# Six tiles of scores in one run, the fourth in the banks of attn @ v

## The chip, the cores and the metric

The kernel runs on one core of a Trainium2 chip. Time is the device time of one execution in microseconds (us); lower is better. The engines are called by their names in the profile: PE (TensorE, the matmuls), PEld (its weight loads), DVE (VectorE), ACT (ScalarE), POOL (GpSimd) and SP (SyncE, which issues the DMAs). SBUF is the working memory, PSUM the memory of eight banks into which matmuls write.

## The reference

All inputs are f32. For each of 8 batches and 12 heads, with 448 rows of 64:

```python
scores = scale * np.matmul(q, k.transpose(0, 1, 3, 2)) - np.log(S)
attn = 1.0 / (1.0 + np.exp(-scores))
out = np.matmul(attn, v)
x = out.transpose(0, 2, 1, 3).reshape(B * S, H * D)     # 3584 x 768
h = np.maximum(x @ moe_w_in, 0.0)                       # 768 x 2048, given as f64
result = (h * h) @ moe_w_out                            # 2048 x 768, given as f64
```

The two weight matrices come as 8-byte numbers and are turned into f32 on the chip.

## The kernel before

The kernel has an attention stage and an MLP stage. The change touches the attention stage and the names of some PSUM banks in the MLP.

**Pairs and blocks.** The 96 heads are 48 *pairs* of two heads, numbered n = 0 to 47; one pair's q and k are one tile x of 128 partitions by 2 x 448 (`load_pair`, 448 KB). `block(ps, d)` works on two pairs, n = 2d and n + 1, for d = 0 to 23. All of the attention stage stands under a manual schedule: on each engine, instructions run in the order in which the program writes them.

**Scores.** To keep f32 accuracy with the faster fp32r matmul, each x is *split* into a high part (a cast, line 254, DVE) and a low part (x minus the high part, line 255, DVE). Scores of a pair (`scores`, line 263) are three tiles of 128 keys by 2 heads by 448 queries. Each tile is two PSUM banks and takes three passes (high x high, low x high, high x low), each pass two matmuls, one for each head, which run side by side (line 272). There are three such tiles in PSUM, tag "sc", six banks. ACT turns every tile into attention weights with a sigmoid (line 260). 448 keys leave a rest of 64 for each pair; `scores_rest` (line 282) computes the rest of the next block's two pairs in one tile, from x that isn't split.

**attn @ v.** `attn_v_rest` (line 293) opens the sums of both pairs in two single banks, tag "single", with the part of the rest; `attn_v` (line 304) adds the three tiles of one pair. `put_x` (line 312) copies a finished sum out of its bank to a tile xo, on DVE for the even pair and on ACT for the odd one (`scalar=True`). For the first two batches xo is kept in SBUF, otherwise it is stored to HBM by a DMA.

**Weights beside it.** Between the scores the f64 weights are converted: `weights_words` (ACT, lines 145 and 146, called words) and `weights_join`, which is either a *join* (three DVE operations at lines 150, 151 and 154, then an add on POOL at line 157) or, each third step, the *sums* of four blocks (DVE, lines 166 to 169) with two stores. The steps are spread over the pairs: step k belongs to pair k * 45 // 43, so nearly each pair has one step. `weights_join` also issues the load of a later chunk. The dictionary `PIECES` adds work at the end of blocks 13, 15, 17, 19, 21, 22 and 23: `make` (pieces 1, 2, 3, 6) splits x operands of the MLP, the high part by ACT (line 327) and the low part by DVE (line 328), in three parts; pieces "t1" to "t3" are three subtractions on DVE (line 353).

**The order of one block before**, d > 0, as each engine sees its part:

```python
put(n - 1, True)                    # ACT copies the odd pair of the block before
score(ps, n, xs[n])                 # PE: three tiles; ACT: three sigmoids
weights_of(weights_join, n - 1)     # DVE, POOL: first slot
split_ahead(n + 2)                  # DVE
rest[d + 1] = scores_rest(...)      # PE, ACT
pav[n], pav[n + 1] = attn_v_rest(...)
score(ps, n + 1, xs[n + 1])         # PE: three tiles more
weights_of(weights_join, n)         # second slot
...                                 # words, stores of xo
attn_v(n, ...); split_ahead(n + 3); attn_v(n + 1, ...)
pieces_of(...); put(n)              # DVE copies the even pair
```

**The MLP.** Two products by Strassen's scheme with seven products each, four groups of tokens. Sums of kind "a" and "b" lie in six banks of a second pool, which takes the room of the score tiles; sums of kind "c" (hc in the first product, oc in the second) lie in the two single banks.

Of the kernel before, what the change touches and what calls it, by code (L numbers as in the profile page):

```python
# [68 lines left out]
def sigmoid_attention_relu2_mlp(  # L69
# [181 lines left out]

    def split_pair(b, p, x):
        hi, lo = op2(f"qh_{b}_{p}", F32R), op2(f"ql_{b}_{p}", F32R)
        nc.vector.tensor_copy(out=hi, in_=x)  # L254
        nc.vector.tensor_sub(out=lo, in0=x, in1=hi.bitcast(F32))  # L255
        return hi, lo

    def sigmoid(name, sc):
# [3 lines left out]

    def scores(ps, b, p, x, passes=((0, 0), (1, 0), (0, 1))):

        out = []
        for t in range(NT):
            sc = ps.tile([P, 2, 512], F32, tag="sc", bufs=3, name=f"sc_{b}_{p}_{t}")[:, :, :S]
            ks = slice(t * P, (t + 1) * P)
            for n, (kp, qp) in enumerate(passes):
                for j in range(2):  # L270
                    rows = slice(j * D, (j + 1) * D)
                    nc.tensor.matmul(  # L272
                        sc[:, j],
                        x[kp][rows, 1, ks],
                        x[qp][rows, 0],
                        start=(n == 0),
                        stop=(n == len(passes) - 1),
                    )
            out.append(sigmoid(f"at_{b}_{p}_{t}", sc))
        return out  # L280

    def scores_rest(ps, d, xs):

        sc = ps.tile([P, 2, 512], F32, tag="sc", bufs=3, name=f"sr_{d}")[:, :, :S]
        for r, x in enumerate(xs):
            for j in range(2):
                rows = slice(j * D, (j + 1) * D)
                nc.tensor.matmul(  # L288
                    sc[r * KR : (r + 1) * KR, j], x[rows, 1, NT * P :], x[rows, 0], start=True, stop=True
                )  # L290
        return sigmoid(f"rest_{d}", sc)

    def attn_v_rest(d, rest, vt):

        pavs = [single(f"pav_{2 * d + r}") for r in range(2)]
        for r in range(2):
            for j in range(2):
                rows, columns = slice(r * KR, (r + 1) * KR), slice(j * D, (j + 1) * D)
                nc.tensor.matmul(  # L299
                    pavs[r][columns], vt[rows, 2 * NT, columns], rest[rows, j], start=True, stop=False  # L300
                )
        return pavs
# [85 lines left out]

    ps1 = ctx.enter_context(tc.tile_pool(name="ps1", bufs=2, space=PSUM))
    warm = op2("warm").rearrange("p a s -> p (a s)").bitcast(BF16)  # L390
# [32 lines left out]

    def block(ps, d):

# [3 lines left out]
        more = n + 2 <= last  # L429
        for m in (n + 4, n + 5):  # L430
            load(m)
# [5 lines left out]
        if d == 0:  # L437
            split_ahead(1)
            score(ps, 0, (x[0],), ((0, 0),))
            rest[0] = scores_rest(ps, 0, (x[0], x[1]))  # L440
            score(ps, 1, xs[1])
        else:
            put(n - 1, True)
            score(ps, n, xs[n])
            weights_of(weights_join, n - 1)
        split_ahead(n + 2)
        if more:
            rest[d + 1] = scores_rest(ps, d + 1, (x[n + 2], x[n + 3]))
        pav[n], pav[n + 1] = attn_v_rest(d, rest.pop(d), vt[d])
        if d > 0:  # L450
            score(ps, n + 1, xs[n + 1])
        weights_of(weights_join, n)
        weights_of(weights_words, n)
        weights_of(weights_words, n + 1)
# [13 lines left out]

    def split_ahead(n):
        if n <= last:  # L470
            xs[n] = split_pair(*pairs[n], x[n])

    def score(ps, n, *args):
        at[n] = scores(ps, *pairs[n], *args)

# [25 lines left out]


    def single(name):
        return ps1.tile([P, 512], F32, tag="single", bufs=2, name=name)[:, :S]

# [11 lines left out]
    def gemm1(g, ops, weights, between):  # L517
# [25 lines left out]
        def run(n, i):  # L543
# [70 lines left out]
    def gemm2(g, blocks, operands1, weights1, ahead):  # L614
# [47 lines left out]
        for at, n in enumerate(order):  # L662
# [5 lines left out]
            for e in range(NE):  # L668
                if n in (1, 7, 2):
                    banks[k, e] = (single if k == "c" and e < 2 else bank)(f"o{k}_{g}_{e}")  # L670
                for i in range(NI):
# [27 lines left out]
    with tc.manual_schedule():  # L699
        with tc.tile_pool(name="ps", bufs=3, space=PSUM) as ps:  # L700
# [8 lines left out]
            for h in range(2):  # L709
                f64[0, h] = load_chunk(*todo[0], h)  # L710
            for d in range(len(pairs) // 2 - 2):
                block(ps, d)
# [4 lines left out]
            block(ps, len(pairs) // 2 - 2)  # L717
# [73 lines left out]
```

## Time and profile before

| | us |
|---|---|
| median of 3 runs | 1080.39 |
| the runs | 1080.41, 1080.39, 1079.15 |
| profiled execution, its own time | 1079.62 |
| its span in the profile | 1077.8 |
| PE busy | 1071.5 |
| DVE busy | 800.7 |
| ACT busy | 610.1 |
| POOL busy | 68.0 |

The profile is one execution; its times count from the first instruction, and what lies between the span and the execution's own time is before and after the program's instructions. A row of the order of time gives the start in us, the length in us, the engine and its line in the kernel, the operation, which tile it writes and which it reads, the size, and how many instructions of the same kind are merged (x2). What stands in brackets at its end is how long the engine had been idle and what released it. A row of a group gives the number of instructions, then the busy time in us, the mean ns of one, and the idle time ahead of them. Lengths of two matmuls overlap, since matmuls are pipelined: the distance from start to start is what a matmul costs. PE busy near 100% therefore doesn't say that PE works at its peak, and a wait of PE shows as a start that comes late.

### The profile page before, as it was taken

To read this page: it belongs to the slowest core of one execution; us is meant where nothing else is said; L and a number is where in the kernel's file an instruction comes from. 1 tells how busy PE (TensorE), PEld (TensorE's weight loads), DVE (VectorE), ACT (ScalarE), POOL (GpSimd) and SP (SyncE) were. 2 spreads that over 40 slices of the span, in tenths; PEclk is the share of its full clock that TensorE was granted. 3 is DMA by queue.
4 is the path that set the end of the run, shared out by engine and by line. 5 is a ranking of instruction groups with operands and counts; after the bars stand their busy time and mean duration, and the time that the engine had idled before them with its cause. 6 is when DMAs were issued, how large, how long until landed. Compare 5 with 4: busy or idle time off the path is not lost.

```text
span 1077.8 us, 14887 instructions
## 1 busy us (share of the span) xinstructions
PE 1071.5 (99%) x5859; PEld 887.3 (82%) x5859; DVE 800.7 (74%) x867; ACT 610.1 (57%) x752; POOL 68.0 (6%) x40
## 2 busy tenths in 40 slices
PE   9999999999999999999999999999999999999998
PEld 4555555546999999999999999999999999999997
DVE  6999899996787996825579975456896935579941
ACT  7888888876555664534454753344565623355721
POOL 1222223220020000000000000000000000000000
PEclk9999999999999999999999999999999999999999
DMA  9989999964654435543343464333345633333441
GB/s 370 387 307 336 347 354 340 352 226 137 228 198 154 143 117 176 194 140 103 103 120 108 127 233 161 110 116 105 90 141 187 209 94 114 123 101 115 143 143 52
DMA packets 82294, 196.80 MB, mean 183 GB/s; under 512 B 6576, under 2 KB 56624, under 8 KB 82224
## 3 DMA queue, kind: packets, MB, share of 16 engines
q1 hardware_dynamic: 82224, 195.85, 52.8%
q8 instruction: 46, 0.75, 0.3%
q14 instruction: 24, 0.20, 0.0%
HBM read 154.53 MB, written 41.29 MB: 182 GB/s over the span
## 4 chain that ended last, share of the span: by engine, by line
PE 91%; DVE 7%; issue 2%; ACT 0%; ACTq 0%; DVEq 0%
PE ha L513 22%; PE oa L513 22%; PE hb L513 11%; PE ob L513 11%; PE pav L308 6%; PE sc L272 6%; PE hc L513 5%; PE oc L513 5%; DVE ql L255 2%; PE sr L288 1%; PE pav L299 1%; DVE qh L254 1%; DVE a L154 1%; DVE a L151 1%; DVE a L150 0%
## 5 line engine op out<-in xcount | busy, mean ns | idle before, releaser
L235 DVE TENSOR_TENSOR w_1l<-w_1l,w_1h 128x1536 fp32r<-128x1536 f32 x60 | 105.3, 1756 | 63.2 <-ACT w_1h L234 62.7
L260 ACT ACTIVATE at<-sc 128x896 f32<-128x896 f32 x144 | 121.8, 920 | 20.8 <-PE sc L272 20.8
L541 ACT COPY s<-ha 128x448 f32<-128x448 f32 x96 | 51.0, 532 | 145.7 <-PE ha L513 131.3
L308 PE MATMUL pav<-at,v 128*64 128x448 f32 x576 | 113.5, 543 | 0.0
L234 ACT CAST w_1h<-w_1l 128x1536 fp32r<-128x1536 f32 x60 | 88.8, 1480 | 19.3 <-DMA w_1l<-w 19.2
L255 DVE TENSOR_TENSOR ql<-x,qh 128x896 fp32r<-128x896 f32 x47 | 94.5, 2011 | 1.7
L308 PEld LDWEIGHTS pav<-at,v 128*64 128x64 f32 x576 | 39.1, 137 | 63.6 <-issue 63.4
L235 DVE TENSOR_TENSOR w_5l<-w_5l,w_5h 128x1152 fp32r<-128x1152 f32 x32 | 43.3, 1355 | 46.5 <-ACT w_5h L234 46.5
L157 POOL TENSOR_TENSOR a<-a,f 128x768 int32<-128x768 int32 x28 | 58.6, 2093 | 177.4 <-ACT xo L315 58.7
L234 ACT CAST w_0h<-w_0l 128x1536 fp32r<-128x1536 f32 x28 | 41.5, 1481 | 47.9 <-DMA w_0l<-w 47.9
L235 DVE TENSOR_TENSOR w_0l<-w_0l,w_0h 128x1536 fp32r<-128x1536 f32 x28 | 49.1, 1754 | 13.5 <-ACT w_0h L234 13.4
L272 PE MATMUL sc<-qh 64*128 64x448 f32 x282 | 56.9, 398 | 0.0
L537 DVE SCALAR_TENSOR_TENSOR g<-g 128x896 f32<-128x896 f32 x48 | 54.1, 1128 | 1.3
L272 PEld LDWEIGHTS sc<-qh 64*128 64x128 f32 x282 | 26.6, 184 | 34.3 <-ACT at L260 15.5
L573 DVE TENSOR_TENSOR g<-hb,s 128x448 f32<-128x448 f32 x32 | 19.9, 622 | 44.7 <-PE hb L513 44.6
L272 PE MATMUL sc<-ql,qh 64*128 64x448 f32 x282 | 51.9, 362 | 0.0
L272 PE MATMUL sc<-qh,ql 64*128 64x448 f32 x282 | 51.7, 361 | 0.0
L234 ACT CAST w_5h<-w_5l 128x1152 fp32r<-128x1152 f32 x32 | 37.1, 1159 | 24.8 <-DMA w_5l<-w 24.8
L659 ACT COPY t<-oa 128x448 f32<-128x448 f32 x36 | 19.1, 530 | 40.1 <-PE oa L513 39.9
L567 ACT ACTIVATE g<-ha 128x448 f32<-128x448 f32 x32 | 17.4, 544 | 33.8 <-PE ha L513 33.8
L513 PE MATMUL oa<-o_2l,w_1h 128*128 128x448 f32 x96 | 35.1, 365 | 0.0
L513 PE MATMUL oa<-o_2h,w_1l 128*128 128x448 f32 x96 | 35.1, 365 | 0.0
(520 smaller groups left out, 3029.8 us busy)
## 6 DMA issues: line engine op xcount, KB each, us to landing
w_1l<-w SPq DMA_DIRECT2D x60, 768.0 KB, 4.4
x<-qk SPq DMA_DIRECT2D x48, 448.0 KB, 6.0
w_0l<-w SPq DMA_DIRECT2D x28, 768.0 KB, 4.5
f<-w_in SPq DMA_DIRECT2D x16, 768.0 KB, 9.2
w_5l<-w SPq DMA_DIRECT2D x32, 384.0 KB, 4.0
v<-v SPq DMA_DIRECT2D x24, 448.0 KB, 6.8
w<-s SPq DMA_DIRECT2D x14, 768.0 KB, 7.8
outT<-o SPq DMA_DIRECT2D x47, 224.0 KB, 2.0
```

The costliest lines, as they stand in the source:

```text
L157: nc.gpsimd.tensor_tensor(out=wb, in0=wb, in1=t.bitcast(I32)[:, :, 0], op=ALU.add)
L234: nc.scalar.copy(out=hi, in_=raw)
L235: nc.vector.tensor_sub(out=lo, in0=raw, in1=hi.bitcast(F32))
L255: nc.vector.tensor_sub(out=lo, in0=x, in1=hi.bitcast(F32))
L260: nc.scalar.activation(at, sc, AF.Sigmoid, bias=NEG_LOG_S, scale=SCALE)
L272: nc.tensor.matmul(sc[:, j], x[kp][rows, 1, ks], x[qp][rows, 0], start=(n == 0), stop=(n == len(passes) - 1),)
L308: nc.tensor.matmul(pav[columns], vt[:, n % 2 * NT + t, columns], at[t][:, j], start=False, stop=(t == NT - 1))
L513: nc.tensor.matmul(out, a[:, c], b, start=first and n == 0, stop=last and n == 2, skip_group_check=True)
L537: nc.vector.scalar_tensor_tensor(out=t, in0=t, scalar=0.0, in1=t, op0=ALU.max, op1=ALU.mult)
L541: nc.scalar.copy(out=s, in_=banks["a", i])
L573: nc.vector.tensor_add(out=tile_of("21", i), in0=out, in1=snaps[2, i])
L659: nc.scalar.copy(out=s, in_=banks["a", e])
```

## The change

It does five things in the attention stage.

- Scores of both pairs of a block come in one run of six tiles, `score(n)` and `score(n + 1)`; the rest of scores, the opening of attn @ v and attn @ v follow.
- The two single banks become one tile of two banks, tag "duo", of which there is one. It holds the sums of attn @ v of both pairs, and, before these are opened, the first tile of the odd pair's scores, the fourth of the run.
- Both copies of x of a block stand in the next block, behind the first slot's join or sums and the first half of a split, and both are on DVE.
- The split is taken apart into `high` and `low`, and goes one pair further ahead: block d splits pairs n + 3 and n + 4 instead of n + 2 and n + 3. In the first slot the two copies stand between high and low. Block 0 splits pairs 1 to 4. Loads of x go one pair further ahead too, with pair 4 loaded ahead of block 0.
- In the MLP, sums of kind "c" take their banks from the same tile of two banks: hc for two products of neighbouring i together, oc for e = 0 and 1.

```diff
-    def split_pair(b, p, x):
-        hi, lo = op2(f"qh_{b}_{p}", F32R), op2(f"ql_{b}_{p}", F32R)
-        nc.vector.tensor_copy(out=hi, in_=x)
-        nc.vector.tensor_sub(out=lo, in0=x, in1=hi.bitcast(F32))
-        return hi, lo
+    def score_tile(name):
+        return ps.tile([P, 2, 512], F32, tag="sc", bufs=3, name=name)[:, :, :S]
 
-    def scores(ps, b, p, x, passes=((0, 0), (1, 0), (0, 1))):
+    def scores(b, p, x, passes=((0, 0), (1, 0), (0, 1))):
...
-            sc = ps.tile([P, 2, 512], F32, tag="sc", bufs=3, name=f"sc_{b}_{p}_{t}")[:, :, :S]
+            sc = (duo if p % 2 and t == 0 else score_tile)(f"sc_{b}_{p}_{t}")
...
     def attn_v_rest(d, rest, vt):
 
-        pavs = [single(f"pav_{2 * d + r}") for r in range(2)]
+        sums = duo(f"pav_{d}")
+        pavs = [sums[:, r] for r in range(2)]
...
-    def block(ps, d):
+    def block(d):
         n = 2 * d
         more = n + 2 <= last
-        for m in (n + 4, n + 5):
+        for m in (n + 5, n + 6):
             load(m)
...
         if d == 0:
-            split_ahead(1)
-            score(ps, 0, (x[0],), ((0, 0),))
-            rest[0] = scores_rest(ps, 0, (x[0], x[1]))
-            score(ps, 1, xs[1])
+            for m in (1, 2, 3):
+                high(m)
+                low(m)
+            score(0, (x[0],), ((0, 0),))
+            rest[0] = scores_rest(0, (x[0], x[1]))
         else:
-            put(n - 1, True)
-            score(ps, n, xs[n])
             weights_of(weights_join, n - 1)
-        split_ahead(n + 2)
+            high(n + 3)
+            put(n - 2)
+            put(n - 1)
+            low(n + 3)
+            score(n, xs[n])
+        score(n + 1, xs[n + 1])
         if more:
-            rest[d + 1] = scores_rest(ps, d + 1, (x[n + 2], x[n + 3]))
+            rest[d + 1] = scores_rest(d + 1, (x[n + 2], x[n + 3]))
         pav[n], pav[n + 1] = attn_v_rest(d, rest.pop(d), vt[d])
-        if d > 0:
-            score(ps, n + 1, xs[n + 1])
         weights_of(weights_join, n)
+        high(n + 4)
+        low(n + 4)
         weights_of(weights_words, n)
         weights_of(weights_words, n + 1)
...
         attn_v(n, pav[n], at[n], vt[d])
-        split_ahead(n + 3)
         attn_v(n + 1, pav[n + 1], at[n + 1], vt[d])
         pieces_of(*PIECES.get(d, ()))
-        put(n)
...
+    def high(n):
+        if n <= last:
+            xs[n] = op2(f"qh_{n}", F32R), op2(f"ql_{n}", F32R)
+            nc.vector.tensor_copy(out=xs[n][0], in_=x[n])
+
+    def low(n):
+        if n <= last:
+            nc.vector.tensor_sub(out=xs[n][1], in0=x[n], in1=xs[n][0].bitcast(F32))
...
-    def single(name):
-        return ps1.tile([P, 512], F32, tag="single", bufs=2, name=name)[:, :S]
+    def duo(name):
+        return ps1.tile([P, 2, 512], F32, tag="duo", bufs=1, name=name)[:, :, :S]
...
-                banks[k, i] = (single if k == "c" else bank)(f"h{k}_{g}_{i}")
+                if k != "c":
+                    banks[k, i] = bank(f"h{k}_{g}_{i}")
+                elif i % 2 == 0:
+                    two = duo(f"hc_{g}_{i}")
+                    banks[k, i], banks[k, i + 1] = two[:, 0], two[:, 1]
...
             for h in range(2):
                 f64[0, h] = load_chunk(*todo[0], h)
+            load(4)
...
-            block(ps, len(pairs) // 2 - 1)
+            block(len(pairs) // 2 - 1)
+            put(last - 1)
             put(last, True)
```

More of the change, by code (lines that the diff above doesn't have):

```diff
@@ L280, in scores, with scores_rest @@
         return out
-    def scores_rest(ps, d, xs):
-        sc = ps.tile([P, 2, 512], F32, tag="sc", bufs=3, name=f"sr_{d}")[:, :, :S]
+    def scores_rest(d, xs):
+        sc = score_tile(f"sr_{d}")
         for r, x in enumerate(xs):
@@ L387, in x_operands @@
         }
-    ps1 = ctx.enter_context(tc.tile_pool(name="ps1", bufs=2, space=PSUM))
+    ps1 = ctx.enter_context(tc.tile_pool(name="ps1", bufs=1, space=PSUM))
     warm = op2("warm").rearrange("p a s -> p (a s)").bitcast(BF16)
@@ L467, in load, with score @@
             x[n] = load_pair(*pairs[n])
-    def split_ahead(n):
+    def high(n):
         if n <= last:
-            xs[n] = split_pair(*pairs[n], x[n])
-    def score(ps, n, *args):
-        at[n] = scores(ps, *pairs[n], *args)
+            xs[n] = op2(f"qh_{n}", F32R), op2(f"ql_{n}", F32R)
[3 more added lines that the diff above has]
+            nc.vector.tensor_sub(out=xs[n][1], in0=x[n], in1=xs[n][0].bitcast(F32))
+    def score(n, *args):
+        at[n] = scores(*pairs[n], *args)
     def put(n, scalar=False):
@@ L669, in gemm2 @@
                 if n in (1, 7, 2):
-                    banks[k, e] = (single if k == "c" and e < 2 else bank)(f"o{k}_{g}_{e}")
+                    if k != "c" or e == 2:
+                        banks[k, e] = bank(f"o{k}_{g}_{e}")
+                    elif e == 0:
+                        two = duo(f"oc_{g}")
+                        banks[k, 0], banks[k, 1] = two[:, 0], two[:, 1]
                 for i in range(NI):
@@ L710, in sigmoid_attention_relu2_mlp @@
                 f64[0, h] = load_chunk(*todo[0], h)
+            load(4)
             for d in range(len(pairs) // 2 - 2):
-                block(ps, d)
+                block(d)
                 if d == KEPT * NP // 2:
@@ L716, in sigmoid_attention_relu2_mlp @@
             load_first(0, False)
-            block(ps, len(pairs) // 2 - 2)
+            block(len(pairs) // 2 - 2)
             load_first(0, True)
```

## The prediction

> **What bounds the kernel now.** I read the busy time of the engines over the attention stage first, then the order of time of TensorE (PE), VectorE (DVE), GpSimd (POOL), ScalarE (ACT) and the DMA queue (SP) in one pair of pairs, a block. In the order of time the columns are start, length in us, engine, line. Only this stage changes its pace; it runs from 16.75 us, the start of block 1, to 256.87 us, the first matmul of the MLP.
>
> ```profile
> 16.75:256.87 240.12, 238.45 (x1742) 123.57 (x1740) 222.57 (x271) 196.31 (x248) 58.61 (x28) 1.00 0.89 329
> ```
>
> The columns after the span are the busy us of PE, its weight loads, DVE, ACT and POOL, then the granted clock, 1.00. PE is full and DVE has 222.57 of 240.12: two engines close to their limit. Block 18 on PE, and the few rows beyond it that I need:
>
> ```profile
> 16.75 0.47 PE L272 MATMUL sc<-qh 64*128 64x448 f32 x2
> ...
> 192.99 0.47 PE L272 MATMUL sc<-qh 64*128 64x448 f32 x2
> 193.29 0.36 PE L272 MATMUL sc<-qh,ql 64*128 64x448 f32 x2
> ...
> 194.70 0.37 PE L272 MATMUL sc<-ql,qh 64*128 64x448 f32 x2
> 195.01 0.98 PE L288 MATMUL sr<-x 64*64 64x448 f32 x8
> 195.81 0.93 PE L299 MATMUL pav<-rest,v 64*64 64x448 f32 x8
> 196.67 0.47 PE L272 MATMUL sc<-qh 64*128 64x448 f32 x2
> ...
> 198.69 4.73 PE L308 MATMUL pav<-at,v 128*64 128x448 f32 x24
> 203.35 0.47 PE L272 MATMUL sc<-qh 64*128 64x448 f32 x2
> ...
> 239.64 0.98 PE L299 MATMUL pav<-rest,v 64*64 64x448 f32 x8 [1.13 <-DVE xo L317]
> ...
> 247.23 0.48 PE L272 MATMUL sc<-qh 64*128 64x448 f32 x2
> ...
> 256.87 0.47 PE L513 MATMUL ha<-x_0h,w_1h 128*128 128x448 f32 x1
> ```
>
> A block takes 203.35 - 192.99 = 10.36 us; the last one, without a rest of scores, 256.87 - 247.23 = 9.64. 22 blocks and the last make 237.6 of 240.1 us, so PE waits some 2.4 us in all now. The row at 239.64 shows what for: a copy of x that DVE made late. That copy may come up to 2.8 us into the next block before PE minds.
>
> DVE beside it, from a join of weight words (line 150 on) to the next group:
>
> ```profile
> 195.26 0.55 DVE L150 TENSOR_SCALAR a<-a 128x768 f32<-128x768 f32 x1
> ...
> 197.31 0.62 DVE L254 CAST qh<-x 128x896 fp32r<-128x896 f32 x1
> 197.97 2.64 DVE L255 TENSOR_TENSOR ql<-x,qh 128x896 fp32r<-128x896 f32 x1
> 200.53 0.55 DVE L150 TENSOR_SCALAR a<-a 128x768 f32<-128x768 f32 x1
> ...
> 205.80 0.61 DVE L317 COPY xo<-pav 128x448 f32<-128x448 f32 x1
> 206.34 0.54 DVE L166 TENSOR_TENSOR s<-a 128x384 f32<-128x384 f32 x1
> ...
> 208.32 0.62 DVE L254 CAST qh<-x 128x896 fp32r<-128x896 f32 x1
> 208.98 1.09 DVE L255 TENSOR_TENSOR ql<-x,qh 128x896 fp32r<-128x896 f32 x1
> 209.99 0.55 DVE L150 TENSOR_SCALAR a<-a 128x768 f32<-128x768 f32 x1
> ```
> ```profile
> 197.63 2.03 POOL L157 TENSOR_TENSOR a<-a,f 128x768 int32<-128x768 int32 x1 [9.04 <-DMA w<-s]
> ```
>
> The subtraction of a split (line 255) takes 1.09 us alone and 2.64 behind a join, where POOL's add is under way until 199.66. So a join with its split costs 200.53 - 195.26 = 5.27 us of DVE, a group of sums with its split 209.99 - 206.34 = 3.65, a copy of x 0.54.
>
> **The gain on PE.** T is the start of a block's scores. Pairs of score matmuls follow each other by (194.70 - 193.29) / 7 = 0.201; the first takes 0.30 (192.99 to 193.29) and the last hands over after 0.31. Two runs of nine pairs cost 2 x 2.02 = 4.04 us, one run of eighteen 0.30 + 16 x 0.201 + 0.31 = 3.83. The rest of scores (0.80), the rest of attn @ v (0.86) and attn @ v (4.66) keep their prices, as a seam is only moved. A block comes to 10.15, 0.21 less: 22 blocks give 4.6 us. Work on weights, x operands and the whole MLP keep their amount; the hc and oc pairs of banks are asked for again only several products (1.8 us each) after their adds, so I cost them at nothing. load(4) ahead of block 0 stays behind the same transfers, and v and the next words go one x-load later (448 KB, 1.4 us at the 329 GB/s of the first row), and are first read in block 1, more than that after they land.
>
> **What the fourth tile waits for.** It lies in the banks of attn @ v, so PE may write it only once both copies of x of the block before are done. It starts at T + 0.30 + 8 x 0.201 = T + 1.91. A copy lasts 0.61, so with a hand-over of under 0.1 the second copy must start by T + 1.23; it can't start before T + 0.1, when attn @ v has ended. Thus the window on DVE shrinks from some 4.5 us (2.3 before T to 2.1 after) to 1.1, and both copies are now DVE's, where ACT took one. Everything after the copy on DVE, and PE's tiles five and six, the rest and attn @ v, queue behind it.
>
> From the start of a join to the second copy it is 2.05 (195.26 to 197.31) + 0.66 + 0.54 = 3.25 us; from the sums 1.98 + 0.66 + 0.54 = 3.18. Behind a join the two copies fill time in which the subtraction stood still for POOL anyway (197.97 to 199.66), so join and split with two copies remain 5.27. This asks that a copy from PSUM runs beside POOL's add. Below is the nearest row: a DVE operation reading PSUM, begun 0.25 us after POOL and not stretched. I take that, at no cost; the other bound, a copy held until POOL ends, moves the second copy by 199.66 + 0.54 - 195.26 - 3.25 = 1.7 us.
>
> ```profile
> 328.06 1.03 POOL L157 TENSOR_TENSOR b<-b,fd 128x384 int32<-128x384 int32 x1 [5.28 <-issue]
> ```
> ```profile
> 328.31 0.62 DVE L573 TENSOR_TENSOR g<-hb,s 128x448 f32<-128x448 f32 x1 [0.38 <-PE hb L513]
> ```
>
> Now from second copy to second copy. After a join in the block's first slot, 5.27 - 3.25 = 2.02 us of that slot remain, after sums 0.54 + 1.01 = 1.55. Steps run sums, join, join, and a block takes two: first slot join, then join, then sums: 2.02 + 5.27 + 3.18 = 10.47; first slot sums, then join, join: 1.55 + 5.27 + 3.25 = 10.07; first slot join, then sums, join: 2.02 + 3.65 + 3.25 = 8.92. Together 29.46 against 3 x 10.15 = 30.45: it fits on the mean. But a join can't start before ACT has read its words, and ACT does these after seven sigmoids:
>
> ```profile
> 193.89 2.54 ACT L260 ACTIVATE at<-sc 128x896 f32<-128x896 f32 x3 [0.26 <-PE sc L272]
> 196.30 0.94 ACT L260 ACTIVATE rest<-sr 128x896 f32<-128x896 f32 x1
> ```
>
> They start at T + 0.90 and follow by (196.30 - 193.89) / 3 = 0.80, so the words begin at T + 6.5 and their first half (0.95, quoted below) is done at T + 7.5, 2.65 before the next T: the second copy comes at T + 0.6 at best, and at T + 0.95 after the 10.47. The deadline is met by 0.3 us. In the plain blocks I cost the waits at nothing, with little to spare.
>
> **Where it doesn't fit.** First, block 1. The split of pair 4 now stands on DVE ahead of its first join, and x of pair 4 is issued at 5.61 and takes 9.5 us in a queue that is full:
>
> ```profile
> 5.61 1.27 SPq L244 DMA_DIRECT2D x<-qk  x2
> ```
> ```profile
> x<-qk SPq DMA_DIRECT2D x1, 448.0 KB, 9.5
> ```
>
> It lands at 15.1; split 1.67, the join starts at 16.8 and the second copy at 20.05, where the deadline is 16.75 + 1.23 = 17.98. PE waits 2.1 us, and in block 2, after 10.47 us of DVE, another 0.3.
>
> Second, the pieces of the x operands at the end of blocks 13, 15 and 19. Their halves are ACT's, behind the words, and DVE's subtractions wait for them, ahead of the next join:
>
> ```profile
> 148.22 0.95 ACT L145 ACTIVATE a<-f 128x768 f32<-128x768 f32 x1
> 149.04 0.93 ACT L146 ACTIVATE f<-f 128x768 int32<-128x768 uint32 x1
> 149.84 1.05 ACT L327 CAST x_0h<-xo 128x448 fp32r<-128x448 f32 x2
> ```
> ```profile
> 150.46 1.16 DVE L328 TENSOR_TENSOR x_0l<-xo,x_0h 128x448 fp32r<-128x448 f32 x2 [1.21 <-ACT x_0h L327]
> ...
> 152.07 0.62 DVE L317 COPY xo<-pav 128x448 f32<-128x448 f32 x1
> ```
>
> The words take 149.84 - 148.22 = 1.62, so the halves start at T + 8.1, DVE 0.62 later, and it is through after 1.61 more (150.46 to 152.07): T + 10.4, the next block's T + 0.2. Then join or sums and the split's first half: second copy at T + 3.4, 2.2 late. Now the same 1.2 us of waiting on DVE costs PE nothing, as the copy then had 2.8 us. Three times 2.2 is 6.6. Third, the subtractions at the end of blocks 17, 21 and the operand of 22 put 1.6 us into the chain: 8.92 + 1.6 or 10.0 + 1.6 against 10.15 leaves 0.3, 0.3 and 0.7 beyond the window: 1.3. Last, in block 23 no rest stands between scores and the banks: PE would be there at T + 3.83, the fourth tile's sigmoid ends at T + 0.90 + 2.4 + 0.92 and hands over at T + 4.3: 0.45 lost against 0.21 won, 0.2.
>
> Sum: -4.6 + 0.2 + 2.4 + 6.6 + 1.3, and -2.4 for the waits of now, which this list replaces: +3.5 us on the profiled execution's 1079.62 (span 1077.8), 1083.1. The median of the runs shown is 0.8 higher; I give 1083.4.
>
> **The rivals.**
> Faster: the piece blocks keep the deadline. Place: second copies of blocks 14, 16, 20. It decides at T + 1.23: should DVE reach the join 2 us sooner than my T + 10.4, the 6.6 fall away: 1076.5. For it: DVE's mean load leaves 1 us in three blocks. Against: the 1.21 us in which DVE waits for ACT now, on the same chain. 0.13.
> No change: half the piece waits, or those of the plain sort, are hidden: 1080, within 2. 0.20.
> Slower still, the 0.3 us margin fails in plain blocks (if the join also waits for the second half of the words, 0.8 later, as its tile is the same): about 0.5 per three blocks, 1087. 0.11.
> The banks show in every block, the copies held by POOL's add: then join and split with two copies cost 5.27 + 2 x 0.54, three blocks 29.46 + 2 x 1.08 = 31.6 us of DVE, 10.54 a block, which bounds them: 22 x 0.39 = 8.6 more, 1092. The row at 328.31 is against it, and the three tiles (1.91 us) ahead of the fourth, which cover a copy and its hand-over (0.7). 0.07. The Trainium skill, "Perfetto Trace Analysis", section "Matmuls", wants independent groups of matmuls to rotate through different PSUM banks, so that one's evacuation overlaps the next one's matmuls; the change goes against that with its fourth tile, and by the rule a copy would be exposed in each block. The trace of before agrees only as far as its 2.4 us of waits go, with two banks that no scores use.
> That the run of six isn't in one piece is hardly a rival: the order on PE is the written one.
>
> **Chances.** The forecast, 1081.5 to 1086, has 0.49; with the cases above the range that leaves out under 2 in 10 is 1077 to 1090. A measurement of this kernel tells about 0.2% (2.2 us) from no change. Faster 0.15 (the first rival and a little of the second), same 0.25, slower 0.60.
>
> **What would show it.** Blocks of 10.15 us where nothing waits (3 to 12). PE waits before the fourth tile, for a copy of x at line 317, of some 2 us in blocks 1, 14, 16 and 20 and no others over 1. DVE waiting for x of pair 4 until 15.1. Line 255 falls from the 94.5 us of the row below to 75 to 80, as behind 14 of the 28 joins the copies take its place in the wait for POOL. Wrong would be: waits in every second block (puts held, or words late), or none after the pieces.
>
> ```profile
> L255 DVE TENSOR_TENSOR ql<-x,qh 128x896 fp32r<-128x896 f32 x47 | 94.5, 2011 | 1.7
> ```

## The result and the profile after

The changed kernel takes 1086.63 us, the median of 6 executions (1084.02 to 1104.06), against 1079.51 us for the kernel before (6 executions, 1079.15 to 1080.41). The ratio is 1.0065, with a 95% interval of 1.0046 to 1.0083: slower, by about 7 us, under 1%. The ratio leaves out the longest execution, which is over 1.5% above the shortest.

The profiled execution spans 1084.4 us, 6.5 more than before. This is the attention stage of the changed kernel, from the first scores of block 1 to the first matmul of the MLP; the columns are the span, busy us of PE, PEld, DVE, ACT and POOL, the granted clock, the DMA share and GB/s.

```profile
17.43:262.18 244.75, 237.62 (x1743) 127.02 (x1741) 215.57 (x292) 182.52 (x225) 58.60 (x28) 0.99 0.88 322
```

The stage grew from 240.12 to 244.75 us, while PE's busy time in it hardly moved (238.45 before). The clock of 0.99 is new. What PE waited for, as the view of waits sums it over the span (us in all, times, the longest):

```profile
PE sc L269 <- DVE xo L315: 6.7, 4, 2.1
...
PE pav L297 <- ACT at L254: 0.5, 1, 0.5
PE hc L517 <- DVE g L566: 0.4, 1, 0.4
PE ha L517 <- DVE w_1l L235: 0.2, 1, 0.2
```

The first row is the fourth tile of scores, waiting for a copy of x at what is now line 315. The four places are blocks 14, 16, 20 and 22. In the order of time of PE, blocks 14 and 16, attn @ v of the plain blocks 18 and 19, and block 22:

```profile
149.88 0.47 PE L269 MATMUL sc<-qh 64*128 64x448 f32 x2
...
151.61 0.37 PE L269 MATMUL sc<-ql,qh 64*128 64x448 f32 x2
154.05 0.47 PE L269 MATMUL sc<-qh 64*128 64x448 f32 x2 [2.08 <-DVE xo L315]
...
174.29 0.37 PE L269 MATMUL sc<-ql,qh 64*128 64x448 f32 x2
176.60 0.47 PE L269 MATMUL sc<-qh 64*128 64x448 f32 x2 [1.94 <-DVE xo L315]
...
177.80 0.63 PE L269 MATMUL sc<-ql,qh 64*128 64x448 f32 x2
178.18 0.63 PE L269 MATMUL sc<-qh 64*128 64x448 f32 x2
...
202.17 4.73 PE L306 MATMUL pav<-at,v 128*64 128x448 f32 x24
212.34 4.73 PE L306 MATMUL pav<-at,v 128*64 128x448 f32 x24
...
243.89 0.47 PE L269 MATMUL sc<-qh 64*128 64x448 f32 x2 [0.62 <-DVE xo L315]
```

A plain block takes 212.34 - 202.17 = 10.17 us; before it was 10.36. In block 14 the fourth tile comes 154.05 - 151.61 = 2.44 after the pair ahead of it, where 0.20 is the rule: 2.24 lost. In block 16 it is 2.11, and then something else follows: pairs of matmuls come 0.38 apart (177.80 to 178.18) in place of 0.20. The granted clock in the slot of that wait, behind it, and behind the wait of block 20 shows why:

```profile
174.12:177.53 3.41, 1.47 (x16) 1.12 (x14) 3.41 (x7) 1.92 (x4) 0.00 (x0) 1.00 0.36 140
177.53:180.94 3.41, 3.41 (x20) 1.96 (x20) 3.31 (x5) 2.73 (x3) 1.30 (x1) 0.50 0.92 303
...
221.90:225.32 3.42, 3.42 (x22) 2.21 (x22) 3.35 (x7) 2.75 (x3) 0.00 (x0) 0.50 0.94 245
```

For 3.41 us after each of these two waits PE's clock is granted at 0.50. Blocks 16 and 20 took 13.94 and 14.01 us: 3.77 and 3.84 over a plain one, 2.11 and 2.18 of it the wait, and 1.66 each the halved clock. Block 14, with a wait as long, took 12.51 and kept its clock; its idle time lies across two slots of the same grid, 1.66 us before 153.64 and the rest behind it:

```profile
150.22:153.64 3.42, 1.75 (x18) 1.29 (x14) 3.35 (x7) 2.54 (x3) 1.20 (x1) 1.00 0.90 378
153.64:157.05 3.41, 3.00 (x30) 2.26 (x34) 3.38 (x6) 2.09 (x3) 0.90 (x1) 1.00 0.82 262
```

The balance of the 6.5 us, from the starts of blocks in the two traces: the shorter run gives 22 x 0.20 = 4.4 and the waits of before 2.4 more; blocks 14, 16 and 20 cost 6.5 in waits and 3.3 in clock, block 22 0.9, blocks 1 and 2 0.3, block 23 0.3 (9.95 for 9.64); block 1 starts 0.7 later; and from the first matmul of the MLP to the end it is 822.2 for 821.0, 1.2 more. In all 13.2 - 6.8 = 6.4.

The other executions carry the mean clock only: 1084.02 us at 1.000, three of 1086.14 to 1086.77 at 0.997, 1089.91 at 0.994. Two stretches of 3.41 us at half clock make 0.997 of a span of 1084. So the changed kernel took 1084.0 us in its one execution at full clock, and the clock adds some 2.5 to its median. The longest, 1104.06 at 0.995, is not explained by the clock; it has no trace, and the last experiment shows what made some other executions long.

### The profile page after: what moved, and what is told of

Its sections match the earlier page's. It is cut to its first block, busy times and chain, and to the rows that moved or that the text cites. A ratio compares the mean times of both kernels' runs of the same rounds, so it can differ in the third digit from the quotient of the medians.

```text
span 1084.4 us, 14883 instructions
## 1 busy us (share of the span) xinstructions
PE 1071.9 (99%) x5859; PEld 890.9 (82%) x5859; DVE 795.7 (73%) x890; ACT 595.0 (55%) x729; POOL 68.0 (6%) x40
## 4 chain that ended last, share of the span: by engine, by line
PE 93%; DVE 2%; ACT 2%; issue 1%; DMA 1%; SPq 0%; DVEq 0%; ACTq 0%
PE oa L517 22%; PE ha L517 21%; PE ob L517 11%; PE hb L517 11%; PE pav L306 8%; PE sc L269 7%; PE oc L517 5%; PE hc L517 5%; PE sr L285 2%; PE pav L297 1%; ACT at L254 1%; DMA f<-w_out 1%; DVE xo L315 1%; PE warm_ps L715 0%; DVE x_0l L326 0%
## 5 line engine op out<-in xcount | busy, mean ns | idle before, releaser
L476 DVE TENSOR_TENSOR ql<-x,qh 128x896 fp32r<-128x896 f32 x47 | 78.0, 1660 | 0.9
L315 DVE COPY xo<-pav 128x448 f32<-128x448 f32 x47 | 27.1, 616 | 13.3 <-PE pav L306 13.2
L517 PE MATMUL oa<-o_1l,w_0h 128*128 128x448 f32 x96 | 35.1, 365 | 0.0
```

The costliest lines, as they stand in the source:

```text
L315: nc.vector.tensor_copy(out=x, in_=pav)
L476: nc.vector.tensor_sub(out=xs[n][1], in0=x[n], in1=xs[n][0].bitcast(F32))
L517: nc.tensor.matmul(out, a[:, c], b, start=first and n == 0, stop=last and n == 2, skip_group_check=True)
```

## The experiments

All are edits of the changed kernel; "before" is the kernel before, which took 1079.8 us in each of these comparisons.

### Both copies on ScalarE

```diff
-            put(n - 2)
-            put(n - 1)
+            put(n - 2, True)
+            put(n - 1, True)
```

> Both copies of x of a block go to ACT, ahead of the sigmoids, and nothing else moves. Theory A (PE waits at the fourth tile because the second copy stands on DVE behind the pieces, a join and half a split, and the clock halves after those waits): the second copy is done at T + 1.1 in every block, no wait before the fourth tile in blocks 14, 16, 20 and 22, granted clock 1.000; the attention stage takes 22 x 10.17 + 9.95 = 233.7 us instead of 244.75, the time comes to about 1075. Rival B (the fourth tile's banks are a bound of their own, whoever copies, and ACT with 0.45 us more a block becomes the limit): sigmoids start 0.2 later, PE waits some 0.3 in most blocks, 1081 or more.

Measured: 1075.03 us (1074.73 to 1075.21), ratio 0.9956, interval 0.9944 to 0.9968. The same window and the waits of PE in this kernel:

```profile
17.60:251.23 233.63, 233.15 (x1742) 124.97 (x1741) 207.35 (x246) 201.31 (x271) 58.86 (x28) 1.00 0.90 337
```
```profile
PE pav L297 <- ACT at L254: 0.5, 1, 0.5
PE hc L517 <- DVE g L566: 0.5, 1, 0.5
```

Beside the start's, which the kernel before has too, and the 0.2 for w_1l, these are all. No wait for a copy is left, in the piece blocks neither, the clock stays at 1.00, and the stage is 233.63 us, 11.1 shorter. The order of time of ACT at the start of block 14 (T = 149.77) shows what changed:

```profile
149.88 0.97 ACT L313 COPY xo<-pav 128x448 f32<-128x448 f32 x2 [0.57 <-PE pav L306]
150.74 4.99 ACT L254 ACTIVATE at<-sc 128x896 f32<-128x896 f32 x6
```

DVE is as late as in the changed kernel, its join starting at T + 0.26 (150.03). But ACT stands idle at T (0.57 us), its first sigmoid being due at T + 0.9 only, and the copies fit in there. So the run of six tiles, the banks and the splits further ahead are sound together; the loss hangs on which engine copies.

### The second copy alone on ScalarE

```diff
             put(n - 2)
-            put(n - 1)
+            put(n - 1, True)
```

> The changed kernel with the second copy of x on ScalarE, the first left on VectorE. Theory A (two readers of the one tile of two banks follow each other, as at the end of attention, where ScalarE's copy began 0.04 us after VectorE's had ended): the second copy ends no sooner, and ScalarE's sigmoids queue behind it, so the waits of blocks 14, 16 and 20 get longer, to some 2.9 us instead of 2.2, and plain blocks lose 0 to 0.3: 1086 to 1092. Rival (the tile lets both read at once, ScalarE's copy is done early and VectorE has one copy fewer): the waits shrink by 0.55 each, to 1.7, too short to halve the clock: 1081.6 us at a clock of 1.000.

Measured: 1092.18 us (six executions, 1091.18 to 1101.5), ratio 1.0127 (1.0102 to 1.0152). Half of the step is worse than none. The profiled execution is the longest, 1101.5 us. Block 14 of its trace, DVE and then ACT:

```profile
156.01 0.61 DVE L315 COPY xo<-pav 128x448 f32<-128x448 f32 x1
```
```profile
156.66 0.53 ACT L313 COPY xo<-pav 128x448 f32<-128x448 f32 x1 [3.96 <-DVE xo L315]
157.08 3.35 ACT L254 ACTIVATE at<-sc 128x896 f32<-128x896 f32 x4
```

ACT's copy starts 0.04 us after DVE's has ended (156.01 + 0.61 = 156.62), though it reads the other bank: in this program two readers of the tile of two banks follow each other. ACT had been held 3.96 us by then with the block's sigmoids behind the copy. Theory A holds, though not by the place it named first: the waits of the fourth tile grow by 0.1 to 0.2 only, to some 2.4. What it loses against the changed kernel's trace, from the starts of blocks: 2.1 in block 1, 1.7 in the plain blocks 3 to 13, which take 10.2 to 10.5, 2.6 in blocks 14, 16 and 20, where this time all three waits halved the clock, 1.35 in block 23, and 0.6 elsewhere, 8.4 in all. Its MLP takes another 7.7 us more than the changed kernel's, since its matmuls follow each other at another pace from 694 us on, which the last experiment looks into. The rival, an early copy and shorter waits, fell.

### The fourth tile out of the banks of attn @ v

```diff
-            sc = (duo if p % 2 and t == 0 else score_tile)(f"sc_{b}_{p}_{t}")
+            sc = score_tile(f"sc_{b}_{p}_{t}")
```

> The changed kernel, but the fourth tile of scores is taken from the three tiles of the others and no longer from the two banks of attn @ v; the copies stay on VectorE. Theory A (the waits of blocks 2, 14, 16, 20 and 22 are the fourth tile's for the copies, and nothing behind it on VectorE is late by itself): these waits are gone (7.9 us), since the banks are first written at the rest of attn @ v, 2.7 us later; and the granted clock stays full. In their place six tiles turn over three: the sixth tile and the rest of scores wait for the sigmoids, which follow each other by 0.80 where TensorE takes 0.60 a tile, so each block is some 0.45 longer, 10.6 us, 22 times 0.45 is 9.9. 1084.0 (the changed kernel at full clock) - 7.9 + 9.9: 1086. Rival (VectorE is late by itself after the pieces, whichever tile waits): blocks 14, 16 and 20 stay at 12.2 or more and the time is 1092 or more.

Measured: 1084.8 us (1084.64 to 1095.87, five executions), ratio 1.0073 (1.0041 to 1.0104). No wait for a copy is left on PE's list, and the clock is 1.000. Here is block 14, now without a wait for a copy, in PE's order of time:

```profile
155.11 0.47 PE L269 MATMUL sc<-qh 64*128 64x448 f32 x2
...
159.43 0.98 PE L285 MATMUL sr<-x 64*64 64x448 f32 x8
160.23 0.93 PE L297 MATMUL pav<-rest,v 64*64 64x448 f32 x8
...
165.75 0.47 PE L269 MATMUL sc<-qh 64*128 64x448 f32 x2
```

It takes 165.75 - 155.11 = 10.64, as expected, and others 10.70: the rest of scores starts 4.32 us after the block instead of 3.84, since tiles turn over no faster than the sigmoids. So nothing behind the copies on DVE is late by itself. The copies of block 14 end 3.5 us into it, where the changed kernel's ended at 4.0; that is still too late for the fourth tile's 1.9, and it costs nothing here, where the banks are asked for at 5.1 us. And the banks are what buys the change its 0.2 us a block: without them the run of six costs 0.3 more than the kernel before.

### The low halves of the pieces behind the copies

The subtractions of pieces 1, 2, 3 and 6 (line 326) go from the end of their block to behind the copies of the next.

```diff
-                split_to(hi, lo, x, vector)
+                if g == 0 and product in (1, 2, 3, 6):
+                    nc.scalar.copy(out=hi, in_=x)
+                    lows.append((hi, lo, x))
+                else:
+                    split_to(hi, lo, x, vector)
...
             low(n + 3)
+            for hi, lo, raw in lows:
+                nc.vector.tensor_sub(out=lo, in0=raw, in1=hi.bitcast(F32))
+            lows.clear()
             score(n, xs[n])
```

> In blocks 13, 15, 19 and 22 the low halves of the x operands, DVE's subtractions, move from the end of the block to behind the copies and the low part of the next block's first slot; ACT's high halves stay. Theory A: DVE no longer waits for ACT ahead of the join, the waits of 2.34, 2.17 and 2.24 us in blocks 14, 16 and 20 go, and with them the half clock (3.2): 1086.1 - 10 = about 1076.5, clock 1.000. Rival C (DVE is simply too full there; the 1.6 us of subtractions push the next copies late wherever they stand): the waits come one block later with 1 us or more each, 1081 or more.

Measured: 1080.32 us (12 executions, 1079.95 to 1096.47), ratio 1.0007 (0.9998 to 1.0016). This lies between the two expectations. The profiled execution is a long one, 1096.07 us, but not through its attention stage: from the first matmul of the MLP to the end it takes 838.2 us where the changed kernel took 822.2, and without these 16.0 it would be at 1080.1, like the median. In its trace blocks 14 and 20 are plain, 10.17, and 16 takes 10.37. But the list of waits has a row, and DVE's order of time shows where one of them went:

```profile
PE sc L269 <- DVE xo L315: 3.6, 3, 1.6
```
```profile
177.76 2.63 DVE L484 TENSOR_TENSOR ql<-x,qh 128x896 fp32r<-128x896 f32 x1
180.31 0.55 DVE L150 TENSOR_SCALAR a<-a 128x768 f32<-128x768 f32 x1
...
182.90 1.15 DVE L315 COPY xo<-pav 128x448 f32<-128x448 f32 x2
```

The subtractions have only gone later on the same engine. Block 17 starts at T = 181.01; DVE comes to its join at 180.31, 0.7 ahead of T, and its copies end at T + 3.0. Blocks 17 and 22 lose 1.4 and 1.9, blocks 16, 18, 19 and 21 0.1 to 0.3 each, and block 1 1.1. So the 1.2 us in which DVE waits for ACT's halves is a good part of the piece waits, not all: the 1.6 us of subtractions have to fit in somewhere, at a mean slack of 1 us in three blocks.

### PE kept at work through the waits

The third tile of the first pair is computed four times over in blocks 14, 16 and 20: 1.84 us of matmuls in what was idle time.

```diff
+            again = 4 if t == NT - 1 and b * NP + p in (28, 32, 40) else 1
-            for n, (kp, qp) in enumerate(passes):
+            for n, (kp, qp) in [*enumerate(passes)] * again:
```

> In blocks 14, 16 and 20 the third score tile is computed four times over instead of once (1.8 us more of matmuls, same values), just where PE otherwise waits 2.2 us for the copy. The waits keep their length in sum, but PE idles 0.4 us instead of 2.2. Theory A (the clock halves because PE idles in those waits): clock 1.000 in all executions, the time 1083 to 1084, as in the one execution of the changed kernel whose clock was 1.000 (1084.02), and a smaller spread. Rival D (the half clock has another cause, the longer mix of the stage): half-clock stretches stay, 1086.5 with the same spread. If the filling itself costs time, 1085 at clock 1.000.

Measured: 1087.22 us (8 executions, 1083.68 to 1098.1), ratio 1.0089 (1.0052 to 1.0126). The median is no answer, as executions differ by more than the effect. In the trace the three blocks take 12.52, 12.39 and 12.21, as long as the waits alone made them, with no half clock; and of the eight executions six had a mean clock of 1.000, against one of six of the changed kernel; the other two had 0.998, as one stretch at half clock gives, wherever it lies. Of the five executions under 1090 us, four had a mean clock of 1.000, three of them at 1083.68, 1083.98 and 1084.46 us, which is the 1084.0 of the changed kernel's one execution at full clock. The fourth, 1088.36, is not explained, nor are the three of 1095.71 to 1098.1, two of them at 1.000. The waits are still there as time; what is gone from most is the halving. It agrees with the halving being due to PE's standing still, without the median to prove it.

### The waits made longer

```diff
             high(n + 3)
+            for _ in range(2 * (d in (14, 16, 20))):
+                nc.vector.tensor_copy(out=xs[n + 3][0], in_=x[n + 3])
             put(n - 2)
```

> The changed kernel with the first half of a split made three times instead of once ahead of the copies of x in blocks 14, 16 and 20: 1.24 us more of VectorE there, so TensorE stands still for about 3.2 us instead of 2.0. Theory A (the clock is halved for 3.41 us after each slot of a fixed grid of 3.41 us in which TensorE stood still for more than some 1.8 us): nearly every one of the three waits now fills such a slot, so two to three stretches at half clock in nearly every run, a mean granted clock of 0.995 to 0.997, and 1084.0 + 3.7 + 1.6 x 2.6: 1092 us, with little scatter. Rival (the halving has nothing to do with how long TensorE stands still there): clocks scattered from 0.994 to 1.000 as in the changed kernel, and 1086.5 + 3.7: 1090.

Measured: four executions, two of 1093.68 and 1093.83 us at a clock of 0.997, two of 1110.52 and 1114.17 at 0.990. Theory A expected little scatter; there is more, and the two long ones, of which there is no trace, stay open. Of the two short ones the clock is at the upper end of theory A's range, the time 1.7 over its 1092, since the waits grew by more than was meant: in block 14 to 4.91 us, not 3.2. DVE's and POOL's rows there:

```profile
152.72 0.62 DVE L474 CAST qh<-x 128x896 fp32r<-128x896 f32 x1
153.38 2.80 DVE L445 CAST qh<-x 128x896 fp32r<-128x896 f32 x2
156.09 1.15 DVE L315 COPY xo<-pav 128x448 f32<-128x448 f32 x2
```
```profile
152.94 2.09 POOL L157 TENSOR_TENSOR a<-a,f 128x768 int32<-128x768 int32 x1 [6.15 <-DVE a L154]
```

Two casts from SBUF, 1.24 us alone, took 2.80 beside POOL's add. For the clock, here are the slots of 3.41 us in and behind the waits of blocks 14 and 16, each with its granted clock:

```profile
154.11:157.52 3.41, 0.14 (x2) 0.17 (x4) 3.38 (x5) 0.00 (x0) 0.91 (x1) 1.00 0.03 11
157.52:160.94 3.42, 3.42 (x19) 2.88 (x19) 3.35 (x7) 1.83 (x2) 0.00 (x0) 0.50 0.92 283
178.00:181.40 3.40, 1.52 (x16) 1.07 (x12) 3.30 (x7) 2.54 (x3) 0.00 (x0) 1.00 0.34 143
181.40:184.80 3.40, 2.00 (x18) 1.74 (x18) 3.33 (x7) 1.08 (x2) 0.00 (x0) 1.00 0.53 154
```

Block 14's wait empties one slot (PE busy 0.14) and the next has half clock. Block 16's wait, 3.3 us of idle time, lies across two slots, 1.9 in the one and 1.4 in the other, and neither is followed by half clock. A wait of 1.94 us in block 16 of the changed kernel, in a single slot, was. So in these traces it is not the length of a wait that decides, but its idle time within one slot of a fixed grid. Where a wait falls on that grid differs from trace to trace.

### Single banks for hc and oc in the MLP

```diff
-                if k != "c":
-                    banks[k, i] = bank(f"h{k}_{g}_{i}")
-                elif i % 2 == 0:
-                    two = duo(f"hc_{g}_{i}")
-                    banks[k, i], banks[k, i + 1] = two[:, 0], two[:, 1]
+                banks[k, i] = (single if k == "c" else bank)(f"h{k}_{g}_{i}")
```

and the same for oc, with a third pool of two banks.

> Only the MLP goes back to two single banks for hc and oc; the attention stage keeps the tile of two banks. Theory A (the tile of two banks makes the odd product wait for the add of the even one, and ACT's last copy wait for DVE's): the wait of 0.6 us before the second hc goes, the part from the first MLP matmul to the end falls from 822.2 to between 821.0 and 821.6, time about 0.6 to 1.2 less than the changed kernel at the same clock. Rival E (the 1.3 us come from late weights and operands alone): it stays at 822.2.

> The changed kernel with both copies of x on ScalarE, as in the run of that name, and beside it the MLP's hc and oc products back in two single banks each. Theory A (the tile of two banks is waited for as a whole, and this delays the second hc product by the addition of the first): from the first matmul of the MLP to the end 821.5 us instead of 822.2, so 1074.3 us, and the wait before hc goes from TensorE's list. Rival (the 0.7 us is the difference of two executions): 1075.0, the MLP stays at 822.2.

Alone: from the MLP's first matmul to the end 1083.08 - 261.60 = 821.5 us in the profiled execution, and the wait of hc is gone from PE's list. The changed kernel took 822.2, as did the five other traces with the tile of two banks whose matmuls keep the same pace (822.2 to 822.4). With both copies on ACT the three shortest executions took 1072.95, 1073.77 and 1074.33, which agrees with the 1074.3 expected but doesn't stand out from the tile of two banks (1073.82 to 1075.21 over ten executions). So far as expected: 0.7 us in the trace. Yet the medians are 1094.52 (10 executions; ratio 1.0101, 1.0064 to 1.0137) and 1089.05 (12; ratio 1.0012, 0.9973 to 1.0052), and of the latter eight took 1087.4 to 1090.4. One took 2456.75, with the matmuls of its trace at more than twice their length and no clock in its record; its cause stays open. What the long ones are is the next run's question.

The first kernel's trace shows block 1 as well, DVE and then PE:

```profile
14.74 0.63 DVE L471 CAST qh<-x 128x896 fp32r<-128x896 f32 x1 [2.59 <-DMA x<-qk]
```
```profile
18.11 0.37 PE L269 MATMUL sc<-ql,qh 64*128 64x448 f32 x2
20.29 0.47 PE L269 MATMUL sc<-qh 64*128 64x448 f32 x2 [1.82 <-DVE xo L315]
```

Here x of pair 4 lands at 14.7 and the fourth tile of block 1 (T = 16.39) loses 1.98 us, and the clock is halved from 21.82 on. In the changed kernel's own trace it landed at 13.65, block 1 started at 17.43, and nothing was lost.

### Both again

The two kernels with ACT's copies, without and with single banks, once more.

> The changed kernel with both copies of x on ScalarE once more, on another chip, for more executions. Theory A (what the changed kernel loses lies in the waits for VectorE's copies, and its MLP runs at the pace of the kernel before): 1075.0 again, no execution over 1078, matmuls of the MLP 202.7 ns apart. Rival (its MLP falls into the pace of 206.7 ns in some executions, as that of other versions did, whose traces show it): 1075.0 in most and 1089 to 1091 in some.

> Both copies of x on ScalarE and single banks for hc and oc once more, of whose executions 3 took 1073 to 1074.3 and 8 took 1087.4 to 1090.4. Theory P (the MLP's matmuls follow each other by 206.7 ns in place of 202.7, from a point near its start on; (206.7 - 202.7) / 202.7 of 821 us is 16.2): executions near 1073.5 or near 1089 and none between, the blocks of attention 10.17 in both, and in a trace of a long one the matmul's distance 206.7 from the start of the MLP. Rival (a wait or a transfer in the MLP that the single banks bring): matmuls 202.7 apart and some 15 us of waits on TensorE's list.

With the tile of two banks: 1074.92 us (1073.82 to 1074.99), ratio 0.9951 (0.9937 to 0.9965). With single banks: 1073.32, 1089.75 and 1090.03. The same 200 us of the MLP of the first and then of the second, of which the profiled execution is a long one:

```profile
300.00:500.00 200.00, 200.00 (x989) 185.38 (x988) 150.71 (x159) 103.45 (x128) 5.12 (x4) 1.00 0.47 153
```
```profile
300.00:500.00 200.00, 200.00 (x970) 181.66 (x969) 147.81 (x156) 102.12 (x126) 5.11 (x4) 1.00 0.47 153
```

989 matmuls against 970 at the same full clock: 202.7 and 206.7 ns from start to start. The attention blocks of the long one are 10.17 us. So theory P holds for the long ones: the whole MLP goes at another pace, 15 us in all, and no wait of PE of such a size shows. The single banks alone don't make it: the MLP of the long execution with the low halves moved, which has the tile of two banks, goes at 206.7 too, as the same 200 us show.

```profile
300.00:500.00 200.00, 200.00 (x969) 181.69 (x968) 149.36 (x161) 100.04 (x125) 6.16 (x5) 1.00 0.47 154
```

In the trace of the single banks the MLP's first matmuls are 203 apart, PE waits 0.2 us for w_1l (the same wait as in the changed kernel), and from the second matmul behind it they are 206 to 207 apart to the end. In the changed kernel's trace four of the six matmuls behind that wait are 206 to 207 apart too, and behind the next wait, the one for hc, 202.7. With the low halves moved it is 202.7 behind the first wait, and from the sixth matmul behind the one for hc on it is 206 to 207 to the end. In the two traces of the kernel with the tile of two banks and ACT's copies it is 202.7 behind both. The kernel before has neither wait. That a wait is what lets the pace change fits these six traces; it was not tried by itself, and one trace (the second copy alone on ScalarE) has 206.7 up to its wait for w_1l, 202.7 behind it, and changes back to 206.7 at 694 us with no wait in the list.

Long executions, 10 us or more above the shortest of the same kernel, are 15 of 24 with single banks (the one of 2456.75 not counted), 10 of 41 with the tile of two banks and one or both copies on DVE, and none of 10 with the tile of two banks and both copies on ACT. Only three of the long ones have a trace that shows the pace, so it is not shown that the others are long for this reason, nor that single banks make them more frequent.

## Why the prediction was right, point by point

The forecast was 1083.4 (1077 to 1090), slower; the measured 1086.63 is in the range and 3.2 above it, and 0.6 above the narrower 1081.5 to 1086 to which it gave 0.49. That the sum came so near is in part luck: on the profiled execution it was 2.5 us too high in two terms (blocks 1 and 2, and the third sort of pieces), while 5.2 us were missing from it (the clock 3.3, the MLP 1.2, a later start of block 1 0.7). The largest term, the waits behind the pieces, was no luck. By its own steps:

- **The gain on PE.** Forecast 10.15 a block and 4.6 in all; measured 10.17 and 4.4. The run of eighteen pairs is 0.20 cheaper, as worked out from the first pair's 0.30 and the last hand-over.
- **The pieces' blocks.** Forecast three waits of 2.2, 6.6; measured 2.24, 2.11 and 2.18, 6.5. The chain was the one named, as the order of time of DVE in the changed kernel shows:

```profile
148.56 1.16 DVE L326 TENSOR_TENSOR x_0l<-xo,x_0h 128x448 fp32r<-128x448 f32 x2 [1.32 <-ACT x_0h L325]
...
150.17 0.55 DVE L150 TENSOR_SCALAR a<-a 128x768 f32<-128x768 f32 x1
...
152.76 1.15 DVE L315 COPY xo<-pav 128x448 f32<-128x448 f32 x2
```

  DVE is through at 150.17, T + 0.3 (forecast T + 0.2), and the second copy starts at T + 3.4 (forecast T + 3.4). The run with ACT's copies shows that it is this wait that costs, the run with the fourth tile elsewhere that it costs only through the banks. The first rival, piece blocks that keep the deadline, fell.
- **Copies beside POOL's add, at nothing.** Right: two copies took 1.15 from 152.76 on, while POOL added from 152.44 to 154.54. All 47 have a mean of 0.62, while casts from SBUF at that place more than doubled. The rival of copies held by POOL fell. The subtraction of the split took the place behind POOL, 78.0 us in all where 75 to 80 were forecast:

```profile
L476 DVE TENSOR_TENSOR ql<-x,qh 128x896 fp32r<-128x896 f32 x47 | 78.0, 1660 | 0.9
L315 DVE COPY xo<-pav 128x448 f32<-128x448 f32 x47 | 27.1, 616 | 13.3 <-PE pav L306 13.2
```
- **Plain blocks without waits, 0.3 to spare.** Right; the rival in which they fail fell.
- **Blocks 1 and 2, 2.4.** 0.3 in this execution, with a block 1 that starts 0.7 later. The wait exists in the form named, 1.98 in another version's trace; its size is a matter of when x of pair 4 lands and when block 1 starts, which move by more than a us from one execution to the next. The four traces of variants that leave this block as it is, with both copies on DVE and the fourth tile in the banks of attn @ v, lose 0.5, 1.1, 1.9 and 2.0 us in it. One trace had been taken for the rule.
- **Blocks 18, 22 and 23, behind the pieces of 17, 21 and 22, 1.3.** Measured 0, 0.9 and 0. How 0.3, 0.3 and 0.7 come out of 8.92 + 1.6 and 10.0 + 1.6, the prediction doesn't show.
- **Block 23, no rest ahead of its sums, 0.2.** 0.3: the price of the wait for the sigmoid (0.46) was right, the win smaller.
- **Missed: the clock.** The sum priced a wait at its length. Two of the three piece waits were followed by 3.41 us at half clock, 1.66 us each: 3.3 us in the profiled execution and the main term of the miss. In its one execution at full clock the changed kernel took 1084.02, 0.6 over the forecast. The Trainium skill, "TensorE: Matmul & The Clock Gate", section "HAM oscillation — how this bites in real kernels", warns of idle gaps of over about 3.4 us; here 1.9 to 2.0 us were enough where they fell within one slot, so the measurement decides. The same page, section "Part 1: The HAM clock gate (the "warmup" mystery)", has a free-running window of 3413 ns, and with this the traces agree: the two half stretches begin at 177.53 and 221.90, 44.37 apart, 13 times 3.413.
- **Mis-sized: hc and oc "at nothing".** 1.2 us. The prediction looked at when a bank is asked for again, and not at what two products or two copies in one tile do to each other. PE's two late starts in the MLP:

```profile
266.71 0.47 PE L517 MATMUL ha<-x_0h,w_1l 128*128 128x448 f32 x1 [0.21 <-DVE w_1l L235]
...
268.85 0.47 PE L517 MATMUL hc<-x_0h,w_1h 128*128 128x448 f32 x1 [0.43 <-DVE g L566]
```

  The second hc product waits for the addition that reads the first one's bank, though its own bank is free; with the seam of PE around it, it starts 0.80 us after the matmul ahead, and the next follows by 0.31, 0.7 over the rule: this is what single banks gave back in their trace. The first row is 0.37 + 0.10 late, 0.5. Ahead of it ACT's copy of the last pair waits for DVE's copy of the pair before from the same tile, and ACT's cast of w_1, from which DVE makes w_1l, stands behind it; no run tried this by itself:

```profile
262.95 0.53 ACT L313 COPY xo<-pav 128x448 f32<-128x448 f32 x1 [4.78 <-DVE xo L315]
263.38 1.48 ACT L234 CAST w_1h<-w_1l 128x1536 fp32r<-128x1536 f32 x1
```

## What to carry over

Giving an operation that PE waits for to an engine that is idle at that moment gained more here than clearing the way for it on the busy one: the same change gives 1.0065 with the copies on DVE, 1.0007 with subtractions moved out of their way, and 0.995 with them on ACT. In this program two banks joined in one tile are waited for as one, by readers as well as by writers, so splitting the readers over two engines makes a chain of them. And a wait of PE should be priced with what the clock does after it, which depends on where it falls.

## What the runs showed of the hardware

- PE's granted clock changes on a fixed grid of 3.41 us: within a trace the half stretches start 44.37 us apart here, 23.89 with the second copy on ScalarE and 71.68 with the waits made longer, 13, 7 and 21 times 3.413. In the traces of this case, slots in which PE was idle for 1.72 us or less were never followed by half clock, those with 1.94 or more always (1.94, 1.99, 2.02, 2.17, 2.97, 3.27); between 1.81 and 1.89 two were and two weren't. So in these traces the bound lies a little over half a slot, and a wait of 3.3 us that two slots shared went free.
- Matmuls of 128x448 in the MLP go at one of two paces, 202.7 or 206.7 ns, at the same full clock, each for hundreds of us: 15 us of this kernel's time. The trace of the kernel before has the shorter one and none of its 50 executions beside the experiments took over 1084.3; of the single-bank versions' executions most were long. The longer pace holds through nearly the whole MLP in one trace with single banks and in one with the tile of two banks, and sets in at 694 us in another. What chooses it is open.
- Beside POOL's add of 2.1 us, DVE's copies from PSUM keep their 0.6 us, while casts from SBUF to SBUF, 0.62 alone, took 2.80 for two.
